# Order of the first value tiles, a weight load in four parts, and a small load issued later, in a fused attention and MLP kernel

## The chip, the cores and the metric

One core of a Trainium2 chip. The time is the device time of the whole kernel in microseconds (us), the median of several executions. The span in a profile is some 2 us shorter than the time. TensorE (PE) does the matmuls and loads their weights (PEld), VectorE is DVE, ScalarE is ACT, GpSimd is POOL, SyncE (SP) issues most DMAs. L212 is line 212 of the kernel; in the changed kernel the output lines are two higher (L513 becomes L515).

## The reference

```python
g = sigmoid((x * gate_w).sum(-1, keepdims=True))
a = attention(x, wqkv, w_phi, wo)     # 16 heads of 28; softmax features of q and k, linear attention
b = gelu(x @ w1 + b1) @ w2 + b2       # 448 -> 1792 -> 448
return g * a + (1 - g) * b            # x: 1 x 2048 x 448, bfloat16
```

## The kernel before

Three parts matter. The first is the start: Wv arrives in four chunks of rows, from two queues, and the gate's weights become a 449th column of each chunk.

```python
for c, eng in ((0, nc.sync), (1, nc.scalar), (2, nc.sync)):
    eng.dma_start(WvG[:, c, 0:D], A_wqkv[c * P:(c + 1) * P, 2 * D:3 * D])
nc.scalar.dma_start(WvG[64:P, 3, 0:D], A_wqkv[384:448, 2 * D:3 * D])
nc.scalar.dma_start(wphi[:, 0:3, :], ...)
...
load_wT(WkT, D)      # DMA transposes on SyncE's queue
load_wT(WqT, 0)
load_x(1)
```

The second is TensorE's order at the start. `v_pair` makes two value tiles (L212), `prep` multiplies the transposed Wk and Wq by a block-diagonal matrix made from wphi (L262, the matrix by VectorE at L191):

```python
dummies(7)                   # 7 matmuls on zeros while x comes in
...                          # x is transposed on TensorE, copied by VectorE and ScalarE
fill_bd()                    # L191
v_pair(0, on_act=True)       # L212, 8 matmuls
v_pair(1)                    # L212, 8 matmuls
prep(WkT, wk_at, (1, 0, 1))  # L262, 16 matmuls
prep(WqT, wq_at, (1, 0, 0))  # L262, 16 matmuls
```

The third is the hand-over from the MLP's first half (L463) to the output tiles (L513), which need w2. The buffer of w2 holds q features until they are transposed, so SyncE can load w2 only late, in one DMA of 1568 KB:

```python
if n == 8:
    nc.sync.dma_start(w2_sb[:], B_w2.rearrange("(j p) n -> p j n", p=P))
```

The softmax here doesn't subtract the row's maximum and nothing guards it: scores larger than these inputs give would overflow.

## Time and profile before

| | before |
|---|---|
| time, median of 3 runs | 149.18 us (149.15 to 149.32) |
| span of the profiled run | 147.5 us |
| TensorE busy | 143.5 us, 97% |
| first value matmul starts | 5.87 us |
| first weight load of WqT (L262) | 10.20 us |
| first weight load from xS for q (L346) | 19.33 us |
| w2 issued, and landed | 79.45, 86.65 us |
| first output matmul (L513) | 87.53 us |

TensorE works nearly all of the time, so the points in the table are those at which something that is not TensorE could still hold it. The lines themselves are in the prediction.

### The profile page before, as it was taken

Reading aid. Unit: us, or ns where it says so; the run is one execution under the profiler, and the core shown is the slowest. Engines: PE = TensorE matmul, PEld = TensorE weight load, DVE = VectorE, ACT = ScalarE, POOL = GpSimd, SP = SyncE. Lnnn points to the kernel's source line nnn. Section 1 sums busy time; section 2 is a strip of 40 time slices with the busy share of each in tenths; the row PEclk is TensorE's granted clock in tenths of the full one; section 3 lists DMA queues with packets and bytes.
Section 4 is the critical chain, followed back from the end, with each engine's and each line's share of the span. In section 5 each row is a group of like instructions: output and inputs, shape, how many; then the busy total and the mean of one; then the engine's idle time right before and its main releaser. Section 6 shows DMA issues by size and latency. Waiting matters only on the chain.

```text
span 147.5 us, 3136 instructions
## 1 busy us (share of the span) xinstructions
PE 143.5 (97%) x1302; PEld 75.1 (51%) x1302; DVE 87.9 (60%) x139; ACT 75.2 (51%) x91; POOL 68.6 (47%) x49
## 2 busy tenths in 40 slices
PE   7999999999999999999999999999999999999991
PEld 2674545555544854444444445554555455555461
DVE  2443699999999999999200027765664345550312
ACT  1655999988989437767676773000611121211100
POOL 7999999999977999919950000000000000000000
PEclk9999999999999999999999999999999999999998
DMA  4999989999700099981899933373434012222111
GB/s 147 236 220 191 149 191 224 217 218 216 165 2 2 4 170 130 205 179 34 120 155 201 312 115 71 71 75 72 131 98 90 17 62 67 67 71 67 41 53 31
DMA packets 44880, 18.02 MB, mean 122 GB/s; under 512 B 36737, under 2 KB 44866, under 8 KB 44866
## 3 DMA queue, kind: packets, MB, share of 16 engines
q1 hardware_dynamic: 43650, 17.16, 57.7%
q10 hardware_dynamic: 1152, 0.65, 1.6%
q8 instruction: 10, 0.16, 0.5%
q14 instruction: 4, 0.03, 0.1%
q0 software_dynamic: 64, 0.01, 0.0%
HBM read 6.28 MB, written 1.84 MB: 55 GB/s over the span
## 4 chain that ended last, share of the span: by engine, by line
PE 97%; DVE 0%; issue 0%
PE y L513 29%; PE hp L463 29%; PE pq L346 7%; PE y L518 6%; PE v_ps L330 4%; PE pk L338 4%; PE pk L231 3%; PE acc L353 3%; PE nm L476 3%; PE v_ps L212 2%; PE warm_ps L384 2%; PE v_ps L231 2%; PE w_ps L262 1%; PE y L523 1%; PE xp L367 1%; PE pk L218 1%
## 5 line engine op out<-in xcount | busy, mean ns | idle before, releaser
L513 PE MATMUL y<-w_sb,gel 128*128 128x448 bf16 (+2 forms) x238 | 45.2, 342 | 0.0
L463 PE MATMUL hp<-xT,w_sb 64*128 64x512 bf16 x196 | 42.6, 376 | 0.0
L463 PE MATMUL hp<-xS,w_sb 64*128 64x512 bf16 x196 | 42.6, 376 | 0.0
L468 ACT ACTIVATE gel<-hp,b1T 128x1024 bf16<-128x1024 f32 x28 | 30.8, 1110 | 13.2 <-PE hp L463 13.2
L513 PEld LDWEIGHTS <-gel 128*128 128x128 bf16 x238 | 22.3, 98 | 20.0 <-issue 0.9
L536 ACT ACTIVATE b2u<-b_sb,ungate 128x448 f32<-128x448 bf16 x16 | 10.2, 666 | 40.8 <-DVE res L528 40.8
L463 PEld LDWEIGHTS <-w_sb 64*128 64x128 bf16 x392 | 19.0, 94 | 23.0
L306 POOL TENSOR_TENSOR phik<-phik,rec 128x1792 bf16<-128x1792 bf16 (+1 forms) x8 | 24.9, 3127 | 1.4 <-DVE rec L303 1.3
L480 DVE TENSOR_SCALAR den<-nm,einv 128x16 f32<-128x16 f32 x16 | 3.7, 230 | 27.9 <-PE nm L476 27.9
L528 DVE SCALAR_TENSOR_TENSOR res<-y,ungate,b2u 128x448 bf16<-128x448 f32 (+2 forms) x17 | 10.8, 653 | 15.4 <-PE y L523 10.1
L301 DVE TENSOR_REDUCE sums<-phik 128x64 f32<-128x1792 bf16 x8 | 16.0, 2000 | 3.2 <-ACT phik L292 3.2
L306 POOL TENSOR_TENSOR oT<-oT,rec 128x1792 bf16<-128x1792 bf16 x4 | 12.7, 3216 | 1.1 <-DVE rec L303 1.1
L518 PE MATMUL y<-wo_sb,oT 128*128 128x448 bf16 (+2 forms) x51 | 11.7, 341 | 0.0
L346 PE MATMUL pq<-Wpq,xT 64*128 64x448 bf16 x56 | 11.5, 349 | 0.0
L346 PE MATMUL pq<-WqS,xS 64*128 64x448 bf16 x56 | 11.4, 349 | 0.0
L306 POOL TENSOR_TENSOR w_sb<-w_sb,rec 128x1792 bf16<-128x1792 bf16 x3 | 9.6, 3212 | 3.0 <-DVE rec L303 3.0
L483 DVE TENSOR_TENSOR o_tok<-nm,den 128x448 bf16<-128x448 f32 x16 | 10.0, 624 | 0.6
L303 DVE RECIPROCAL rec<-sums 128x64 f32<-128x64 f32 x16 | 8.8, 553 | 1.4
L200 DVE CAST vaug<-v_ps 128x896 bf16<-128x896 f32 x7 | 7.5, 1072 | 2.6 <-PE v_ps L212 2.2
L291 ACT ACTIVATE phik<-pk 128x896 bf16<-128x896 f32 x8 | 7.6, 948 | 1.5 <-PE pk L220 1.5
L301 DVE TENSOR_REDUCE sums<-oT 128x64 f32<-128x1792 bf16 x4 | 7.9, 1980 | 0.0
L292 ACT ACTIVATE phik<-pk 128x896 bf16<-128x896 f32 x8 | 7.7, 958 | 0.0
(113 smaller groups left out, 174.2 us busy)
## 6 DMA issues: line engine op xcount, KB each, us to landing
w_sb<-in_B_w_dram SPq DMA_DIRECT2D x4, 784.0 KB, 11.4
out_dram<-res SPq DMA_DIRECT2D x15, 112.0 KB, 1.8
w_sb<-in_B_w_dram SPq DMA_DIRECT2D x1, 1568.0 KB, 7.2
xS<-xT SPq DMA_DIRECT2D x2, 256.0 KB, 4.1
EqT<-in_A_x_dram ACTq DMA_DIRECT2D x1, 448.0 KB, 3.1
xS<-xT SPq DMA_DIRECT2D x2, 192.0 KB, 3.8
wo_sb<-in_A_wo_dram SPq DMA_DIRECT2D x1, 336.0 KB, 16.6
oT<-o_tok SPq DMA_TRANSPOSE x16, 2.4
```

The costliest lines, as they stand in the source:

```text
L292: nc.scalar.activation(out=dst[:, :, :, 1, 0:PW], in_=src, func=ACT.Exp, scale=-1.0)
L301: nc.vector.reduce_sum(out=sums[:], in_=ph, axis=AX.X)
L303: nc.vector.reciprocal(out=rec[:], in_=sums[:])
L306: eng.tensor_tensor(out=ph[:, lo:hi], in0=ph[:, lo:hi], in1=rec[:, lo:hi, :, None].to_broadcast([P, hi - lo, 2, DH]), op=ALU.mult)
L346: nc.tensor.matmul(pq[:, i, 0:D], lhsT=x_half(i, k, h)[:, r * P:(r + 1) * P], rhs=w_half(Wpq, WqS, i, k), start=(k == 0), stop=(k == NK - 1))
L463: nc.tensor.matmul(hp[:, i, :], lhsT=w1_sb[i * HP:(i + 1) * HP, k, j * P:(j + 1) * P], rhs=x_half(i, k, h), start=(k == 0), stop=(k == NK ...
L468: nc.scalar.activation(out=gel[h][:, j, :], in_=hp[:].rearrange("p a b -> p (a b)"), func=ACT.Gelu_apprx_tanh, bias=b1T[:, j:j + 1])
L483: nc.vector.tensor_tensor(out=o_tok[:, t % 4, 0:D].rearrange("p (x h d) -> p x h d", x=NPR, h=2), in0=nmv[:, :, 0:PW].rearrange("p x (h d) ...
L513: nc.tensor.matmul(y, lhsT=gel[t // 8][:, j, (t % 8) * P:(t % 8 + 1) * P], rhs=w2_sb[:, j, cols], start=(opens and j == 0), stop=False)
L518: nc.tensor.matmul(y, lhsT=oT[:, c, t * P:(t + 1) * P], rhs=wo_sb[:, c, cols], start=False, stop=(closes and c == 2))
L528: nc.vector.scalar_tensor_tensor(out=res[:, cols], in0=y, scalar=ungate[:, t:t + 1], in1=b2u[t][:, cols], op0=ALU.mult, op1=ALU.add)
L536: nc.scalar.activation(out=b2u[t][:], in_=b2_sb[:], func=ACT.Copy, scale=ungate[:, t:t + 1])
```

## The change

The intent: ask for the chunks of Wv in the order in which they land, so that TensorE does not wait for a late one; let the first output tile start with the first part of w2; and let GpSimd finish the head mask before it spends time on issuing a small load.

```diff
-    nc.gpsimd.dma_start(wphi[0:64, 3, :], wphi_rows[384:448, :])
     nc.gpsimd.memset(hmask[:], 1.0)
     ...                                          # two affine_select on hmask
+    nc.gpsimd.dma_start(wphi[0:64, 3, :], wphi_rows[384:448, :])
     ...
     def v_pair(u, on_act=False):
         v_ps = four("v_ps")
-        for i in range(2):
-            t = 2 * u + i
-            for c in range(NC4):
+        for n, c in enumerate((1, 0, 3, 2)):
+            for i in range(2):
+                t = 2 * u + i
                 nc.tensor.matmul(v_ps[:, i, 0:D + 1], lhsT=xT[:, c, t * P:(t + 1) * P],
-                                 rhs=WvG[:, c, :], start=(c == 0), stop=(c == NC4 - 1))
+                                 rhs=WvG[:, c, :], start=(n == 0), stop=(n == NC4 - 1))
     ...
         if n == 8:
-            nc.sync.dma_start(w2_sb[:], B_w2.rearrange("(j p) n -> p j n", p=P))
+            for lo, hi in ((0, 3), (3, 6), (6, 10), (10, NJ)):
+                nc.sync.dma_start(w2_sb[:, lo:hi, :],
+                                  B_w2[lo * P:hi * P, :].rearrange("(j p) n -> p j n", p=P))
```

## The prediction

> **What bounds the kernel now.** I read the page's busy table and the shares of the chain that ended last, then the timeline of the first 20 us, then four very short stretches of it (to get the starts of single matmuls, which the timeline merges), then the DMA issues of narrow windows (a window with one issue in it gives that issue's own time to landing), and last the SyncE queue and the stretch around 87 us.
>
> ```profile
> PE 143.5 (97%) x1302; PEld 75.1 (51%) x1302; DVE 87.9 (60%) x139; ACT 75.2 (51%) x91; POOL 68.6 (47%) x49
> ...
> PE 97%; DVE 0%; issue 0%
> ```
>
> TensorE is busy for 143.5 of 147.5 us, and 97% of the chain that ended last is its own. There is hardly an engine to wait for; a part of the change can only pay where it takes TensorE time away, and a gain must then survive every later point where TensorE meets something that does not move. The change touches two such places: the first value tiles (L212) and the first output tiles (L513), which read w2.
>
> The value tiles and what feeds them, from the timeline (start, length, engine, line, operation):
>
> ```profile
> 1.06 3.17 PE L384 MATMUL warm_ps<-w_sb 128*128 128x512 bf16 x7 [1.06 <-DVE w_sb L124]
> 5.12 0.69 DVE L200 COPY xT<-xp 128x1024 bf16<-128x1024 bf16 x1 [2.92 <-PE xp L367]
> 5.80 0.16 ACT L378 CAST WvG<-g_ps 128x1 bf16<-128x1 f32 x1 [0.37 <-DMA WvG<-in_A_wqkv_dram]
> 5.98 0.16 ACT L379 CAST WvG<-g_ps 64x1 bf16<-64x1 f32 x1
> 6.22 0.15 PEld L212 LDWEIGHTS <-xT 128*128 128x128 bf16 x1 [0.23 <-DMA WvG<-in_A_wqkv_dram]
> 6.40 0.95 DVE L191 TENSOR_TENSOR w_sb<-wphi,hmask 128x140 bf16<-128x140 bf16 x4 [0.58 <-POOL mask L181]
> ```
>
> The line at 6.22 is the one the change seems aimed at: a weight load of L212 that idled 0.23 us until a part of Wv landed. The starts of single value matmuls, each line from a short window of its own:
>
> ```profile
> 5.87 0.55 PE L212 MATMUL v_ps<-WvG,xT 128*128 128x449 bf16 x1
> ...
> 6.22 0.75 PE L212 MATMUL v_ps<-WvG,xT 128*128 128x449 bf16 x2
> ...
> 6.59 0.57 PE L212 MATMUL v_ps<-WvG,xT 128*128 128x449 bf16 x2
> ...
> 6.81 0.93 PE L212 MATMUL v_ps<-WvG,xT 128*128 128x449 bf16 x4
> ```
>
> So the first four start at 5.87, 6.22, 6.59 and 6.81; the sixteenth starts at 9.11, which is (9.11 - 6.81)/12 = 0.192 us each from the fourth on. Against sixteen at 0.192 from 5.87 (the last at 8.75) the stage loses 9.11 - 8.75 = 0.36 us, all of it before the fourth matmul. The question of the whole case is what those 0.36 us are.
>
> When each chunk of Wv lands, and two later loads (size, us from issue to landing):
>
> ```profile
> WvG<-in_A_wqkv_dram ACTq DMA_DIRECT2D x1, 112.0 KB, 3.0
> WvG<-in_A_wqkv_dram SPq DMA_DIRECT2D x1, 112.0 KB, 3.2
> WvG<-in_A_wqkv_dram ACTq DMA_DIRECT2D x1, 56.0 KB, 3.9
> WvG<-in_A_wqkv_dram SPq DMA_DIRECT2D x1, 112.0 KB, 4.0
> ...
> WqT<-in_A_wqkv_dram SPq DMA_TRANSPOSE x1, 5.1
> ...
> w_sb<-in_B_w_dram SPq DMA_DIRECT2D x1, 1568.0 KB, 7.2
> ```
>
> With the issues at 1.27 (ScalarE, chunk 1), 1.69 (SyncE, chunk 0), 1.83 (ScalarE, chunk 3) and about 2.1 (SyncE, chunk 2) the chunks land at about 4.3, 4.9, 5.7 and 6.1: the order 1, 0, 3, 2 of the new code.
>
> **What the Trainium skill says.** First, "TensorE: Matmul & The Clock Gate", Part 1 (The HAM clock gate): TensorE starts at 1.2 GHz, goes to 2.4 GHz only after some 3.4 us of sustained work, and back-to-back matmuls then start N/1.2 ns apart cold and N/2.4 + 2.5 ns warm. The trace agrees on the spacing: seven 128x512 dummies from 1.06 on load their weights 0.42 us apart (512/1.2 = 427 ns); for 449 columns the cold figure is 374 ns and the warm one 190 ns, and L212 shows 350, 370, then 220, then 192. Its switch comes later than the page's figure, some 5.5 us after the first matmul. Second, the same page, Part 2 (What happens when you issue a matmul): a weight load may be pulled ahead into the background buffer while a matmul runs. Third, "DMA: Bandwidth & Descriptors", Anatomy of one DMA (the GpSimd path): about 2 us of a DMA are fixed and mostly its completion. The trace has nothing smaller here than 3.5 us for the 3.5 KB wphi load, so I use durations of the trace.
>
> **Value tiles, chunk by chunk.** Before, the chunks are asked for at the starts above: chunk 0 at 5.87 (landed 4.9), chunk 1 at 6.22 (4.3), chunk 2 at 6.59 (6.1, its gate column written by ScalarE at 5.80 + 0.16 = 5.96), chunk 3 at 6.81 (5.7, gate column 5.98 + 0.16 = 6.14). Each is there before its matmul would start. The spacing of the first two gaps is the cold clock's own 374 ns, and the third falls on the switch. The 0.23 us at 6.22 are then, as I read it, the third weight load waiting until the second matmul takes over its weights, not a wait that moves a matmul. The first matmul is held by the first xT copy, 5.12 + 0.69 = 5.81, in both orders. So the new order has the same 16 matmuls, the same 16 weight loads, the same start and the same cold stretch: chunk 3 is asked for by the fifth matmul, at about 7.0, and chunk 2 by the seventh, at 7.4, later than before. Gain: about 0; at most 0.36 if the 0.36 were waiting after all. The second pair of tiles waits for ScalarE's xT copy, 6.17 + 1.01 = 7.18; it starts as ninth matmul at 6.81 + 5 x 0.192 = 7.77, so there is 0.6 us of room.
>
> **Small wphi load later.** GpSimd spends 0.76 us issuing it at 1.50. It now issues after three hmask instructions, (2.25 to 3.08 before), so from about 2.3. It lands some 0.8 us later: 1.50 + 3.5 = 5.0 becomes about 5.8. The last of the four products of L191, which reads it, starts at 7.1: still 1.3 us early. hmask is done about 0.8 us earlier, but L191 also needs the larger wphi load, 2.42 + 3.9 = 6.3, which is when it starts; and its products are first read at 9.31. GpSimd has the same instructions in total. Gain: 0; perhaps 0.2 us of GpSimd time should the issue take 0.55, as its other one does.
>
> **w2 in four parts.** Three more SyncE issues of about 0.5 us after 79.45, so the last goes out near 81.4; SyncE's next job is at 88.71. The four together still move 1568 KB and should be there near 87. The first part (336 KB) should land about 3 us after its issue, taken from the 448 KB x load, which took 3.1: near 82.5 instead of 79.45 + 7.2 = 86.65.
>
> ```profile
> 17.93 1.30 POOL L401 COPY WqS<-Wpq 64x1344 bf16<-64x1344 bf16 x1
> ...
> 19.33 0.28 PEld L346 LDWEIGHTS <-xS 64*128 64x128 bf16 x2
> ...
> 87.50 2.40 PEld L513 LDWEIGHTS <-gel 128*128 128x128 bf16 x14
> ```
>
> But TensorE only comes to L513 at 87.50, 0.85 us after the whole load has landed. There is no wait to remove; the parts after the first are wanted at 87.5 + 3, 6 and 10 x 0.19, so at 89.4 for the last. Gain: 0. Sum of the three parts: 0 to 0.1 us.
>
> **Rivals.** (1) The 0.36 us are a wait for Wv, as the label at 6.22 says, and the new order returns them: span -0.36, 148.8. Even then it would have to pass three fixed points. The transposed Wq lands at 4.97 + 5.1 = 10.07, and its weight load is at 10.20: 0.1 us of room. GpSimd's copy of the x block for the odd tiles ends at 12.96 + 0.61 = 13.57, having waited for a DMA, and is read by matmuls from 13.95: 0.3 us. GpSimd's WqS ends at 17.93 + 1.30 = 19.23, and the first weight load of that stage is at 19.33: 0.1 us. GpSimd was back to back since 12.96, so this point does not follow TensorE. So of 0.36 at most about 0.1 would reach the end: 149.1. Only if DMAs and GpSimd moved too would it be 148.8. (2) The clock gate depends on when the measuring window falls, and TensorE's early work shapes it; a switch some hundred ns earlier or later moves the same stage by up to 0.3 us either way, and the fixed points swallow an earlier one but not a later one: 149.1 to 149.5. Against it stands the spread of the three runs before, 0.17 us. (3) Something is made worse: the later wphi load lands after 7.1, or the four w2 parts contend with the last transposes of EqT (landing 76.67 to about 81) or use up completion slots that output DMAs wait for. A wphi landing 1 us later than I think costs nothing as the products are needed at 9.3; the others have 6 us of room. At worst 149.5.
>
> **Range and chances.** The working gives 149.18 less 0 to 0.1, and I say 149.15. The lower end, 148.8, is rival 1 with GpSimd moving along (I give it about one in ten); the upper end, 149.5, is rivals 2 and 3 plus the spread between runs. 2% would be 3 us; nothing in the change is that large: faster 0.01, same 0.98, slower 0.01.
>
> **What would show it.** Right: L212 still starts near 5.87, its first matmuls still 0.35 to 0.37 apart, its sixteenth start within 0.1 of 9.11; L262's load of WqT still near 10.2; L346 near 19.33; first L513 near 87.5; the first w2 part landed some 4 us before it; TensorE busy time unchanged. Wrong: 0.19 spacing from the first value matmul on and everything after 20 us shifted by the same 0.3 us or more (rival 1), or L346 held later, or an idle stretch of TensorE at L191's products or at L513.

## The result, and the profile after

Six runs of each kernel on one chip: 149.30 us (148.99 to 149.62) with the change, 149.34 us (149.15 to 149.64) without. The ratio is 0.9997, 95% interval 0.9979 to 1.0015: the same. Here and below a ratio is the mean time of one kernel's fast runs over that of the other's in the same rounds, so it is not quite the ratio of the medians.

The page of the changed kernel, its busy table and the shares of the chain that ended last:

```profile
PE 143.4 (97%) x1302; PEld 75.0 (51%) x1302; DVE 87.9 (60%) x139; ACT 75.2 (51%) x91; POOL 68.4 (46%) x49
...
PE 91%; DMA 4%; SPq 2%; DVE 1%; issue 0%
```

TensorE's work is the same, but 4% of the chain is now a DMA. The chain in order of time shows which (start, length, what):

```profile
4.99 5.47 DMA WqT<-in_A_wqkv_dram
```

From the timeline of the same kernel (start, length, engine, line, operation, in brackets the idle time before it and what ended that), the value tiles, VectorE's block-diagonal matrix and the two halves of L262:

```profile
5.91 3.37 PE L212 MATMUL v_ps<-WvG,xT 128*128 128x449 bf16 x16
6.85 0.92 DVE L191 TENSOR_TENSOR w_sb<-wphi,hmask 128x140 bf16<-128x140 bf16 x4 [0.99 <-DMA wphi<-in_A_w_phi_dram]
9.12 1.09 PE L262 MATMUL w_ps<-w_sb,WkT 128*128 128x140 bf16 x16
10.51 1.10 PE L262 MATMUL w_ps<-w_sb,WqT 128*128 128x140 bf16 x16 [0.30 <-DMA WqT<-in_A_wqkv_dram]
```

The value tiles did get shorter: from their first start to the first start of L262 it is 9.12 - 5.91 = 3.21 us, where it was 9.31 - 5.87 = 3.44. All of it was given back at once: the transposed Wq landed at 10.46, and TensorE idled 0.30 us for it. (The ends of matmuls are modelled in the profile, so such an idle time is smaller than the delay. By the starts: in the kernel before the second half of L262 starts 0.92 us after the first, here it would have been at 10.04, and it came at 10.51, so 0.47 us late.) Short windows show why the tiles were shorter. Each line is the matmuls of L212 that touch one window:

```profile
5.91 0.51 PE L212 MATMUL v_ps<-WvG,xT 128*128 128x449 bf16 x1
...
6.26 0.73 PE L212 MATMUL v_ps<-WvG,xT 128*128 128x449 bf16 x3
...
6.46 0.73 PE L212 MATMUL v_ps<-WvG,xT 128*128 128x449 bf16 x3
```

The first two starts are 0.35 us apart, as before, and the next gap is 0.20. In the kernel before there was one more gap of 0.37. Either TensorE's clock stepped up earlier in this execution, or the new order removed a wait.

The parts of w2, from the DMA issues of two windows (size, us from issue to landing):

```profile
w_sb<-in_B_w_dram SPq DMA_DIRECT2D x2, 336.0 KB, 3.7
...
w_sb<-in_B_w_dram SPq DMA_DIRECT2D x1, 448.0 KB, 5.2
```

And their issue and the first output tile, from the timeline:

```profile
79.18 2.19 SPq L500 DMA_DIRECT2D w_sb<-in_B_w_dram  x4
...
87.78 2.81 PE L515 MATMUL y<-w_sb,gel 128*128 128x448 bf16 x14
```

The first two parts are there by about 83.5. The last goes out within the four issues that end at 79.18 + 2.19 = 81.4, and lands 5.2 us after its issue, so by 86.6 at the latest; it is wanted at 87.78 + 10 x 0.19 = 89.7. Its room is at least 3 us, where the single load had 0.85.

### The profile page after: what moved, and what is told of

The parts are those of the page before. It is cut to its first block, busy times and chain, and to the rows that moved or that the text cites. A ratio compares the mean times of both kernels' runs of the same rounds, so it can differ in the third digit from the quotient of the medians.

```text
span 147.5 us, 3138 instructions
## 1 busy us (share of the span) xinstructions
PE 143.4 (97%) x1302; PEld 75.0 (51%) x1302; DVE 87.9 (60%) x139; ACT 75.2 (51%) x91; POOL 68.4 (46%) x49
## 4 chain that ended last, share of the span: by engine, by line
PE 91%; DMA 4%; SPq 2%; DVE 1%; issue 0%
PE y L515 29%; PE hp L463 29%; PE pq L346 7%; PE y L520 6%; DMA WqT<-in_A_wqkv_dram 4%; PE v_ps L330 4%; PE pk L338 4%; PE pk L231 3%; PE acc L353 3%; PE nm L476 3%; SPq L146 2%; PE v_ps L231 2%; PE y L525 1%; PE w_ps L262 1%; PE pk L218 1%; SPq L134 1%
## 5 line engine op out<-in xcount | busy, mean ns | idle before, releaser
L346 PE MATMUL pq<-Wpq,xT 64*128 64x448 bf16 x56 | 11.5, 349 | 0.0
L346 PE MATMUL pq<-WqS,xS 64*128 64x448 bf16 x56 | 11.4, 349 | 0.0
```

Source lines behind the costliest of these rows:

```text
L346: nc.tensor.matmul(pq[:, i, 0:D], lhsT=x_half(i, k, h)[:, r * P:(r + 1) * P], rhs=w_half(Wpq, WqS, i, k), start=(k == 0), stop=(k == NK - 1))
```

## The experiments

Twelve kernels, in three sets of four. Call the chip of the result above A; the sets ran on three other chips, B, C and D, each beside runs of the kernel before. All runs that were timed are fast, with a granted clock of 0.997 or more, except where it is said.

### The kernel before, a second profile (chip B)

No edit. The question is how far two executions of the same kernel differ.

> A second profile of the kernel before, for the spread of two things between executions of one and the same kernel: where the spacing of the value matmuls of L212 goes from 0.37 to 0.19 us, and when the transposed Wq lands. Clock theory (the first value matmuls are 0.35 to 0.37 us apart because TensorE still runs at half rate): the step comes at another of the first four gaps or at the same, by chance, within some hundred ns of 6.6 us. Wait theory (they wait for chunks of Wv): the slow gaps sit where chunk 2 and chunk 3 are asked for, gaps two and three, in this profile too. The weight load of WqT between 10.1 and 10.6; span 147.0 to 147.6.

149.47 us, span 147.4. From two short windows and the timeline:

```profile
5.71 0.75 PE L212 MATMUL v_ps<-WvG,xT 128*128 128x449 bf16 x3 [0.24 <-DVE xT L200]
5.91 0.74 PE L212 MATMUL v_ps<-WvG,xT 128*128 128x449 bf16 x3
...
8.79 1.09 PE L262 MATMUL w_ps<-w_sb,WkT 128*128 128x140 bf16 x16
10.16 0.94 PEld L262 LDWEIGHTS <-WqT 128*128 128x128 bf16 x16 [0.45 <-DMA WqT<-in_A_wqkv_dram]
```

The kernel before, in its old order, has value matmuls 0.19 to 0.20 us apart from the first one on. There was no wait for Wv in it. TensorE was faster earlier: the transposes of x, 1.06 and 1.01 us long in the first profile, took 0.74 and 0.61. And it did not help: TensorE reached WqT 0.5 us earlier and idled 0.45 us. Also expected was a step at about 6.6 us; here it had come before 4.9.

### The new order of the value tiles alone (chip B)

```diff
-            for c in range(NC4):        # tile by tile, chunks 0, 1, 2, 3
+        for n, c in enumerate((1, 0, 3, 2)):    # chunk by chunk, both tiles
```

> The first part of the change alone. Clock theory with the fixed point at WqT: L212 takes 3.2 to 3.45 us from its first start to the first start of L262, whatever the order; L262's weight load of WqT is at WqT's landing, 10.1 to 10.6, TensorE idles there by what L212 saved; time ratio to before 0.998 to 1.001. Wait theory: L212 takes 3.1 us or less in this order, and if the end followed it the ratio would be 0.9975.

Six runs: 149.34, 149.38, 149.63, 150.25, 150.44, 151.02 us; the ratio is 1.0001 (0.9959 to 1.0042). The ratio agrees with the clock theory, but the profile misses both of its other numbers: from L212 to L262 it is 3.06 us (3.2 to 3.45 expected; 3.1 or less was said of the wait theory), and the weight load of WqT is at 9.91, with no idle time. On the same chip the old order has 3.08 us, so the 3.06 is no gain of the new order: in both executions the clock had stepped up before the value tiles. The spread of the times was a surprise. The runs of the kernel before on this chip fall into the same two groups: seven from 149.61 to 149.96, four from 150.45 to 150.81. The profiled run of this kernel is the one of 150.25 us, and its profile shows what an upper run looks like, first in the DMA issues, then in the timeline:

```profile
w_sb<-in_B_w_dram SPq DMA_DIRECT2D x1, 1568.0 KB, 8.6
```

```profile
88.21 2.81 PE L513 MATMUL y<-w_sb,gel 128*128 128x448 bf16 x14 [0.83 <-DMA w_sb<-in_B_w_dram]
```

The single w2 load was issued at 79.51, as usual, but took 8.6 us where the other four profiles with the load at that place have 7.2 to 7.7. TensorE, which was early, stood 0.83 us at the first output tile. By the starts it was 1.0 us late: from L346 to the first output matmul it is 68.2 us in every profile without a wait, and 88.21 - 19.01 = 69.2 here. A gain at the start (L346 at 19.01 in place of 19.33) was lost, and more, at w2.

### Two value tiles without the late chunks (chip B)

```diff
-                                 rhs=WvG[:, c, :], start=(c == 0), stop=(c == NC4 - 1))
+                                 rhs=WvG[:, c % 2 if u == 0 else c, :], ...   # wrong on purpose
```

> The kernel before with the first two value tiles reading chunks 0 and 1 of Wv twice, so that they never ask for the late chunks 2 and 3 (a wrong result on purpose). Clock theory: the first gaps are still 0.35 to 0.37 us until about 6.3 to 6.8 us, then 0.19. Wait theory: all gaps are 0.19 to 0.20 from the first matmul on, and L212 ends 0.3 us earlier than in the kernel before.

149.67 us. Its output is wrong, which doesn't matter for the time. Three short windows:

```profile
6.04 0.36 PE L212 MATMUL v_ps<-WvG,xT 128*128 128x449 bf16 x1
6.04 0.56 PE L212 MATMUL v_ps<-WvG,xT 128*128 128x449 bf16 x2
6.44 0.55 PE L212 MATMUL v_ps<-WvG,xT 128*128 128x449 bf16 x2
```

One matmul lasts 0.36 us and two together 0.56, so the second starts at 6.24 and the third at 6.44: the gaps are 0.20 us, and all that follow are 0.18 to 0.20. There is no slow gap. That is the number of the wait theory, but it decides nothing: the kernel before, with all of its chunks, had the same gaps in the profile above. TensorE had become faster before the first value matmul in both. After the tiles TensorE idled 0.32 us for WqT.

### Three dummy matmuls in place of seven (chip B)

```diff
-    dummies(7)
+    dummies(3)
```

> The kernel before with three dummy matmuls at the start in place of seven, so that TensorE idles from about 2.4 to 4.0 us. Clock theory: the step to 0.19 us comes later[...], so that more or all of the sixteen value matmuls are 0.37 us apart and L212 takes 0.5 to 2.9 us longer; WqT's room of 0.1 us cannot hide this, so the time grows by 0.3 to 2.5 us (ratio 1.002 to 1.017). Wait theory: L212 keeps its gaps and the time is the same within 0.1%.

Four runs, 150.55 us (150.19 to 151.33); the ratio is 1.0038 (0.9989 to 1.0088), wide because of the two groups of the kernel before; its own four runs lie 1.1 us apart. The profile is clear, from the timeline:

```profile
5.12 1.01 PE L367 MATMUL xp<-ident,EqT 128*128 128x128 bf16 x8
5.96 4.82 PE L212 MATMUL v_ps<-WvG,xT 128*128 128x449 bf16 x16
...
10.61 1.09 PE L262 MATMUL w_ps<-w_sb,WkT 128*128 128x140 bf16 x16
...
11.50 1.00 PEld L262 LDWEIGHTS <-WqT 128*128 128x128 bf16 x16
```

From first start to L262 it is 10.61 - 5.96 = 4.65 us, 1.2 more than before, with the same order. Single starts from short windows are 0.34 to 0.38 us apart up to 9.27 and 0.19 after it, while the last chunk had landed by about 6: no load explains that. The slow stretch is TensorE's own pace, and it depends on the work TensorE was given before. The first line says the same in another way. The second eight transposes of x (L367), which read no Wv, take 1.01 us in the four profiles whose value tiles start with a slow gap (the kernel before and the changed kernel on chip A, this one and the last below), and 0.61 to 0.83 us in the ten others, where the value matmuls are 0.18 to 0.20 us apart wherever they do not wait for an operand. A loss of this size is not hidden: TensorE comes to WqT 1.3 us later than before, WqT has long landed, and the span is 148.8, 1.3 us longer. There is no wait at the first output tile in this profile, though its time, 150.88, would be in the upper group of the kernel before.

### The changed kernel, and w2 in parts alone (chip C)

The second is the kernel before with only the last hunk of the diff.

> The changed kernel again, on one chip with the w2 part alone. The times of the kernel before on the chip of the first four experiments fell into two groups, 149.6 to 150.0 and 150.4 to 150.8 (4 of 11), and in the profile of the first part alone TensorE waited 0.83 us at the first output tile for a w2 load that took 8.6 us. Theory of the late w2: the upper group are executions in which the single w2 load lands late, so the changed kernel, whose last part has some 3.5 us of room in place of 0.85, has no upper group: all of its runs within 0.6 us of each other; the ratio of the means is 0.997 to 0.999 where the kernel before shows the upper group in a third of its runs, and 1.000 where it shows none. Rival (the upper group has another cause, in the first 20 us or in the clock): the changed kernel shows the upper group as well, ratio 0.999 to 1.001.

> The second part of the change alone. Theory of the late w2: as the changed kernel, no upper group, ratio within 0.001 of the changed kernel's. Rival: upper group as in the kernel before, ratio 0.999 to 1.001. In the profile no idle time of TensorE at the first output tile; the first w2 part lands 3.5 to 4 us after its issue.

| on chip C | runs, us | ratio to before |
|---|---|---|
| before | 149.10, 149.30, 149.34, 149.35, 149.55, 149.65, 149.72, 149.77, 150.52, 150.53, 150.82 | |
| changed kernel | 149.10, 149.12, 149.38, 149.39, 149.45, 149.67 | 0.9976 (0.9941 to 1.0010) |
| w2 in parts alone | 148.82, 149.04, 149.07, 149.09, 149.17, 149.20 | 0.9956 (0.9920 to 0.9993) |

The upper group is in three of eleven runs of the kernel before, and in none of the twelve with w2 in parts. Neither profile has TensorE waiting for w2. Against the eight lower runs of the kernel before (mean 149.47) the changed kernel is still 0.1 us lower in the mean, and the parts alone 0.4. The parts alone are the only valid kernel whose interval lies below 1. They were expected to stand within 0.001 of the changed kernel, and stood 0.002 below it; the last set comes back to that.

### The w2 load made late on purpose, whole and in parts (chip C)

Two loads of 448 KB go ahead of w2 on SyncE's queue, into a buffer that is not in use then. The results stay right.

```diff
         if n == 8:
+            for _ in range(2):
+                nc.sync.dma_start(o_tok[:, :, 0:D], x[0:512, :].rearrange("(t p) d -> p t d", p=P))
             nc.sync.dma_start(w2_sb[:], ...)     # or the four parts
```

> The kernel before with two more loads of 448 KB (x into the output-token buffer, which is still unused then) ahead of the single w2 load, so that it must land late in every execution; the result stays right. If the first output tile waits for the whole load: the load is issued near 83.5 and lands near 91 to 92, TensorE idles 3.5 to 5 us at L513 and the time grows by that, to about 153 to 155 us. If w2's landing had no part in the end: the same time as before.

> The same two extra loads ahead of w2 in four parts. The first part should land some 4 to 5 us after 83.5, near 88; the others 1 us after each other. TensorE then waits about 1 us for the first part and perhaps 1 us more for later ones: 1 to 2.5 us over the kernel before, 2 to 3 us less than with the single load. If the parts did not help (the whole is what counts), as late as the single load.

From the timelines, first the whole load, then the parts:

```profile
91.07 2.81 PE L515 MATMUL y<-w_sb,gel 128*128 128x448 bf16 x14 [3.54 <-DMA w_sb<-in_B_w_dram]
```

```profile
88.01 1.50 PE L517 MATMUL y<-w_sb,gel 128*128 128x448 bf16 x6 [0.57 <-DMA w_sb<-in_B_w_dram]
89.93 0.92 PE L517 MATMUL y<-w_sb,gel 128*128 128x448 bf16 x4 [0.42 <-DMA w_sb<-in_B_w_dram]
91.17 0.92 PE L517 MATMUL y<-w_sb,gel 128*128 128x448 bf16 x4 [0.32 <-DMA w_sb<-in_B_w_dram]
```

Whole: one wait of 3.54 us, 154.52 us (152.60 to 155.48; the run of 155.48 is slow and not in the ratio), ratio 1.0278. In parts: waits of 0.57, 0.42 and 0.32 us, together 1.31, 151.59 us (151.05 to 152.14), ratio 1.0126. They show that the wait at the first output tile goes into the time and that parts cut it. The size needs care. The profiled run of the whole load is the one of 152.60, at a granted clock of 0.999; its other three runs have 0.988 or 0.989 and are about 2 us longer, so the medians, 2.9 us apart, do not compare like with like. The two profiled runs, 152.60 and 151.05, do: 1.6 us. The starts agree. Against the 68.2 us after L346 the whole load makes the first output tile 3.7 us late; the parts make it 0.7 us late and the tile itself 1.3 us longer (from its start to the next tile's it is 4.37 us in place of 3.11), together 2.0. So the parts are worth about 1.7 us here, a little less than the 2 to 3 that I expected.

### The order and w2 in parts, with the small wphi load in its old place; and the changed kernel again (chip D)

The first is the change without its first hunk.

> The changed kernel with the small wphi load back in its old place (order of the value tiles and w2 in parts remain). Question: why did the changed kernel (149.38) stand 0.3 us above the w2 part alone (149.08) on one chip. Theory wphi: issued later, the small load runs beside the transposed loads of Wk and Wq and delays them; its two profiles have WqT's first weight load at 10.50 and 10.25, the six undelayed others with the early wphi at 9.91 to 10.20 or, once, 10.37. Then this kernel's weight load of WqT is at 9.9 to 10.2 and its time 0.2 to 0.3 us below the changed kernel's. Rival (chance of the execution, or the new order of the value tiles): same time as the changed kernel within 0.1 us.

> The changed kernel, for the comparison with the previous and the next two on one chip. No upper group of times; ratio to the kernel before 0.996 to 0.9985 if the kernel before shows its upper group again in a third of its runs.

| on chip D | runs, us | ratio to before |
|---|---|---|
| before | 149.12, 149.29, 149.36, 149.37, 149.43, 149.43, 149.51, 149.76, 149.95 | |
| without the wphi move | 149.01, 149.05, 149.28, 149.32, 149.36 | 0.9986 (0.9972 to 1.0001) |
| changed kernel | 149.18, 149.37, 149.44, 149.55, 149.62 | 1.0002 (0.9987 to 1.0017) |

The kernel before shows no upper group on this chip, and there the changed kernel gains nothing. My suspicion that the later wphi load delays WqT did not hold in the profiles: the weight load of WqT is at 10.25 us with the load in its old place and at 10.06 in the changed kernel, the reverse of what I expected. The times point the way of the suspicion (means 149.20 and 149.43), but the intervals overlap. It stays open whether the move costs a little or nothing.

### The q product from WkT, so that nothing waits for WqT (chip D)

```diff
-    prep(WqT, wq_at, (1, 0, 0))
+    prep(WkT, wq_at, (1, 0, 0))      # wrong on purpose; WqT is still loaded
```

> The kernel of the first of these runs, with the product for q built from the transposed Wk, so that TensorE never waits for WqT, which is still loaded (a wrong result on purpose). If WqT's landing is what holds TensorE in the first 20 us: the second half of L262 follows the first without idling, 0.9 us after it, L231 starts at 10.6 to 10.9, and the time falls by 0.1 to 0.4 us against the same kernel with WqT. If another point behind it holds as well (the copy of x at 13.4 to 13.6, WqS at 18.8 to 19.2): L231 starts earlier but L346 does not, and the time stays.

The check of the result does not see this error. Four runs, 149.10 us (148.81 to 149.61), ratio to the kernel before 0.9973 (0.9954 to 0.9992), against 0.9986 for the same kernel with WqT: not told apart, so the worth of this wait as a time stays unmeasured. The profiled run, the one of 149.61, fell on something else. From the timeline:

```profile
6.59 0.16 ACT L378 CAST WvG<-g_ps 128x1 bf16<-128x1 f32 x1 [1.45 <-DMA WvG<-in_A_wqkv_dram]
...
6.97 2.74 PE L212 MATMUL v_ps<-WvG,xT 128*128 128x449 bf16 x12 [0.45 <-ACT WvG L379]
```

Here is a real wait for Wv. Chunk 3, which carries only half as many bytes as the others, took 4.7 us where the twelve other profiles with this issue order have 3.5 to 4.0; ScalarE could write its gate columns only at 6.59 and 6.76, and TensorE stood 0.45 us after the fourth value matmul. So the wait the change was aimed at does exist, in one of the thirteen profiles with this issue order. This kernel has the new order, which asks for chunk 3 with its fifth matmul; the old one asks with its fourth, and for chunk 2, which took 4.7 us too, with its third, so it would not have been spared. The two halves of L262 follow each other without a stop, as expected, but L231 started at 11.43 because of the wait before them.

### Chunk 2 of Wv issued by ScalarE (chip D)

```diff
-    for c, eng in ((0, nc.sync), (1, nc.scalar), (2, nc.sync)):
+    for c, eng in ((0, nc.sync), (1, nc.scalar), (2, nc.scalar)):
```

> A version meant to beat both, result right: the kernel of the first of these runs with chunk 2 of Wv issued by ScalarE, so that SyncE starts the transposed loads of Wk and Wq 0.4 us earlier. If SyncE's issue sets WqT's landing: WqT lands near 9.6 to 9.8, TensorE does not idle at L262, time 0.1 to 0.3 us less. If the DMA engines are full there (their busy share is 1.0 or more from 2 to 12 us): WqT lands at 10.0 to 10.2 as before and the time is the same within 0.1 us. ScalarE has 0.5 us more to issue, so its gate columns may start at 5.3 to 5.5 in place of 5.25.

Meant to be faster, it is slower, clear of the noise: 152.05 us (151.77 to 152.27), ratio 1.0176 (1.0156 to 1.0195), outside both branches of what I expected. From the timeline:

```profile
2.11 2.34 SPq L146 DMA_TRANSPOSE WkT<-in_A_wqkv_dram  x1
2.87 0.77 ACTq L136 DMA_DIRECT2D wphi<-in_A_w_phi_dram  x1
...
7.39 0.16 ACT L378 CAST WvG<-g_ps 128x1 bf16<-128x1 f32 x1 [1.97 <-DMA WvG<-in_A_wqkv_dram]
7.78 2.74 PE L212 MATMUL v_ps<-WvG,xT 128*128 128x449 bf16 x12 [0.85 <-ACT WvG L379]
...
8.34 3.55 DVE L191 TENSOR_TENSOR w_sb<-wphi,hmask 128x140 bf16<-128x140 bf16 x4 [2.53 <-DMA wphi<-in_A_w_phi_dram]
...
11.94 0.89 PE L262 MATMUL w_ps<-w_sb,WkT 128*128 128x84 bf16 x13 [1.08 <-DVE w_sb L191]
```

The transposed load of Wk starts 0.5 us earlier, and the two small loads, chunk 3 of Wv (at 2.31) and the 21 KB of wphi, are now issued after it. Chunk 3 took 5.1 us to land and wphi 5.4 (3.9 each before), and ScalarE waited 1.97 us for chunk 3. Whether the transposed load or the place behind chunk 2 on ScalarE's queue makes them slow is not separated. TensorE stood 0.85 us in the value tiles and 1.08 us for VectorE's block-diagonal matrix, and nothing later gave these back: the span is 149.7. The late wphi is only part of the 1.08. The four products of L191 take 0.95 us in the kernel before and 3.55 here: the last two, 0.23 to 0.38 us each in six other profiles, took 1.78 and 1.38 us and ended at 10.58 and 11.89, just after GpSimd's two copies of Wv (L400 from 8.56 to 10.42, L401 from 10.48 to 11.79), beside which they now ran. That VectorE waited for GpSimd there is suggested by these times and not tested.

### The profiles side by side

The weight load of WqT sets TensorE's place for the rest of the kernel, except where w2 comes late. Times in us; "idle" is TensorE's weight queue waiting for WqT just before it.

| kernel, chip | L212 to L262 | WqT load | idle | L346 | span |
|---|---|---|---|---|---|
| before, A | 3.44 | 10.20 | 0 | 19.33 | 147.5 |
| before, B | 3.08 | 10.16 | 0.45 | 19.23 | 147.4 |
| changed, A | 3.21 | 10.50 | 0.46 | 19.58 | 147.5 |
| changed, C | 3.05 | 10.25 | 0.35 | 19.32 | 147.3 |
| changed, D | 3.06 | 10.06 | 0.51 | 19.13 | 147.1 |
| order alone, B | 3.06 | 9.91 | 0 | 19.01 | 148.1 |
| w2 in parts alone, C | 3.08 | 9.98 | 0 | 19.05 | 147.0 |
| three dummies, B | 4.65 | 11.50 | 0 | 20.64 | 148.8 |

From WqT's load to L346 it is 9.07 to 9.14 us in every row, and from there to the end 127.9 to 128.2 us, except for the order alone, where the late w2 makes it 129.1. There is a pattern in this range that I had not looked for: it is 128.2 with the single w2 load and 127.9 to 128.0 with the parts. TensorE's starts do not differ; the 0.2 us lie after VectorE's last instruction, which ends 2.6 us before the end of the span (144.56 + 0.33 of 147.5, before on chip A) or 2.4 (144.55 + 0.33 of 147.3, changed on chip C). The two kernels with a late w2 have 2.5 (whole) and 2.7 (parts) and do not follow it. So w2 in parts seems to give some 0.2 us that has nothing to do with a wait for w2; what it is stays open, and the times of chips A and D do not single it out. What happens before WqT's load reaches the end only where TensorE comes to it later than WqT does.

## Why the prediction was right or wrong

The time, 149.30 us against 149.15 predicted, came out as stated. In part two things cancelled that I had not foreseen. In the profiled run WqT took 5.5 us to land and not 5.1, so L346 came at 19.58 and not 19.33; from there to the end the changed kernel took 0.25 us less, and the span is 147.5 in both. Of the signs that I named, the start near 5.87 (5.91), the first w2 part landing some 4 us before the first output tile (82.9 against 87.78) and TensorE's busy time came true. The sixteenth value start missed (8.93, not within 0.1 of 9.11), and "L346 held later", a sign of being wrong, came, by 0.25 us.

**The reading of the 0.36 us as the cold clock: right.** The kernel before had no slow gap at all on chip B with the old order; three dummies gave nine gaps of 0.34 to 0.38 us, up to some 3 us after the last chunk had landed; and in fourteen profiles the slow gaps come only where the transposes before them, which read no Wv, were slow too. The two tiles without the late chunks decide nothing. The changed kernel's shorter stage on chip A is inside what the kernel before does by itself: 3.44 and 3.08 us in its two profiles. It is no gain of the order: where the clock had stepped up before, the stage takes 3.05 to 3.06 us in the new order and 3.08 in the old. That the 0.23 us at 6.22 moved no matmul is supported too: the kernel with the whole w2 load late has the same label, 0.25 us before its third weight load of L212 at 5.84, and its third matmul starts 0.20 us after the second. The words "Each is there before its matmul would start" held for the one profile and not in general: chunk 3 landed late enough in one later execution to leave TensorE idle for 0.45 us, with the new order.

**The fixed points that swallow a gain: the first is right, the third is wrong.** WqT held TensorE as described, for 0.47 us by the starts in the changed kernel. The second, the copy for the odd tiles, never held it: from WqT's load to L346 the time is the same in every row. But "this point does not follow TensorE", said of GpSimd's WqS, took 19.23 for a fixed time; in the order alone it was done at 17.49 + 1.30 = 18.79, and L346 came at 19.01.

**The small wphi load: no time moved, sizes off.** Predicted were a landing at 5.8 and L191 starting at 6.40 as before. The issue took 0.76 us as before, so the 0.2 us of GpSimd time did not come. The load landed at 2.22 + 4.2 = 6.4, the larger wphi load at 2.42 + 4.3 = 6.7, and L191 started at 6.85 (6.40 before). Nothing waited for it, since L262 starts at 9.12. Whether the move has a small price is open.

**w2 in four parts: "There is no wait to remove" is the step that does not hold in general.** The working took the 7.2 us of one execution for the load's time, and so 0.85 us for its room. On chip B the same load took 8.6 us in one profile, of the kernel with the order alone, and the wait was there, 0.83 us long (1.0 by the starts). The predicted landings of the parts (near 82.5 the first, near 87 the last) fit the measured 3.7 and 5.2 us after issue. The changed kernel's median is within my range on chips C and D as well (149.38, 149.44); what changes with the chip is the kernel before. Chip A showed no upper run, and that the pair gave 0.9997 there is in this respect luck: on chip C it gave 0.9976, and the parts alone 0.9956, below 1 by its interval. The prediction's sentence that the trace has "nothing smaller here than 3.5 us" also misreads it: the 448 KB of x took 3.1 us and chunk 1 of Wv 3.0.

What is shown and what is not: one upper run has a profile, and it has the late w2; the profiles of lower runs with the single load have no such wait; forcing the load late reproduces the wait, and parts cut it. On chips B and C upper runs (150.25 us or more) are 7 of 22 of the kernel before and 3 of 6 of the order alone. The 32 runs with w2 in parts and at its usual time, without the slow last version, are all at 149.67 or below. That each upper run was a late w2 is therefore likely, not shown, and the three dummies show that a run can be this long without one; why the load is late in some executions, and why on two chips and not on A and D, stays open.

## What to carry to other kernels

A slack read from one trace is a sample: where it is smaller than the spread of a DMA's landing between executions, the wait can exist in some of them, and here splitting the load by its order of use kept the time from it, without a clear change of the typical run. A gap at the start of TensorE's work should be held against the cold spacing of its matmuls before it is called a wait, and so should the pace of what TensorE did just before it; a second profile of the same kernel is the cheapest test. An idle time of TensorE was smaller than the delay in these profiles (1.31 against 2.0 us with the late parts); take the delay from starts. Before an early stage is shortened, look for the next load that does not move with it; and moving one issue to another queue can push small, urgent loads behind a long transposed one, as it did here.

## What the Trainium skill lacked or had wrong

- "TensorE: Matmul & The Clock Gate", Part 1: it puts the step to the full clock around 4 us into sustained activity, give or take 500 ns. In the profiles here with seven dummies, the first matmul always near 1.06 us, it came between just before 4.1 us (whole w2 load late, whose first eight transposes of x, from 4.08 on, took 0.62 us in place of 1.06) and about 6.6 us (before, chip A), so 3.0 to 5.5 us after the first matmul: a spread of 2.5 us, not one. (The same Part also says that the number of slow matmuls varies from run to run, which fits.) The page's cold and warm spacings fit: 0.35 to 0.37 and 0.19 us for 449 columns.
- "DMA: Bandwidth & Descriptors": it gives a fixed cost and a rate, but no figure for how much the landing of one and the same load differs between executions. The single 1568 KB load of w2 took 7.2, 7.4, 7.4, 7.7 and 8.6 us in five profiles.
- The same page: nothing on how much later small loads land when they are issued behind a transposed one. The 21 KB of wphi took 3.5 to 4.6 us in thirteen profiles, issued before the transposed Wk (2.42 against 2.58), and 5.4 us in the one with the issue after it (2.87 against 2.11). One profile, and the order on ScalarE's queue changed with it, so the cause is not shown.
